# Strassen's scheme for the last product of a chain of attention and two MLPs

## The chip, the cores and the metric

One core of a Trainium2 chip runs the kernel. Time is the device time of one execution in microseconds (us); the median of the runs counts. TensorE multiplies, VectorE (DVE) and ScalarE (ACT) work on what comes out of it, GpSimd (POOL) helps early on, and SyncE (SP) issues the transfers.

## The reference, cut to what matters

```
x = attention(q, k, v, s)          # 2304 tokens, 512 wide
h = x @ moe_w_in                   # 2304 x 2048
x = (h * cos(h)) @ moe_w_out       # 2304 x 512
h = max(x @ w1, x @ w2, x @ w3)    # three products, 2304 x 768
out = h @ moe2_w_out               # 2304 x 512: the change is here
```

## The kernel before

A planner (class `Plan`) collects operations with an engine, a duration, a key, and the memory spans that they read and write; it plays them on a clock of its own and writes out each engine's instructions in the order of that play. On the chip each engine then works through its list in that order. POOL has nothing left to do in the stage of the change.

**The three products** `x @ w1`, `x @ w2`, `x @ w3` run as 27 groups, `GROUPS` = (fp, tp, m): fp is one of three pairs of d_ff chunks (128 wide), tp one of three pairs of token tiles (`TB` = 384 tokens), m the weight. I number them 0 to 26; fp is slowest, m fastest. Each is a 2 x 2 block product done by Strassen's scheme in 7 sub-products (`product`, L1341), each of 6 matmuls of 384 columns: two chunks of d_model times three terms, since every operand is kept as an f16 high half and an f16 low half (`halves`, L508: ACT writes the high one, DVE the low one). ACT copies three of the sub-products out of PSUM (`keep`), DVE forms the four quarters `q` of the result from banks and copies (`result`, L1375), and for m > 0 takes the maximum with what is there (L1379, L1370). The seventh sub-product of a group (`step_p4`) is placed after the second of the next group. A sub-product that opens no bank of its own adds to one whose earlier content was read first, so TensorE waits for that read.

**The last product** is before plain. When all three m of an (fp, tp) are done, `step_p4` splits the four quarters into halves: two ACT and two DVE instructions of 768 columns (L511 and L514). `final(i)` (L1297) makes 128 rows of the output from 18 matmuls of 512 columns, 6 chunks times 3 terms; there are 18 of them, the last cut in two column halves. A bank is copied out by ACT (`evac`, L904) with the output's scale, and SP stores it. The finals of the first two token pairs stand between the groups of fp = 2, the last eight behind the last group.

`w_operands` and `out_operands` make the weights' halves; `x_operands` the activations'. `combine` (L1120, its DVE instruction L1128) is one sum or difference of two f32 blocks.

Of the kernel before, what the change touches and what calls it, by code (L numbers as in the profile page):

```python
# [332 lines left out]
def attn_moe_kernel(ctx, tc, qT, kT, v, s, w_in, w_out, w1, w2, w3, wo2, out):  # L333
# [23 lines left out]
    def dspan(name, i=0):  # L357
        return (name, Plan.CELL * i, Plan.CELL * (i + 1))
# [750 lines left out]
    wo2_b = [w1_b.sub(2048 * f, 2048) for f in range(NC2)]  # L1109
    h2_b.update({(2, 0): w1_b.sub(2048 * NC2, HB), (2, 1): xo_b.sub(0, HB), (2, 2): xo_b.sub(HB, HB)})  # L1110
    assert 2048 * NC2 + HB <= WB and 2 * HB <= XB
    val2_b = Buf(nc, tail0, 2048 * NC2).ring(NC2)
    junk_b = Buf(nc, one_b.lo, 1024)
    ob_b = raw_all[0].ring(2)

    gate_scale()

# [82 lines left out]
    def out_values(key):  # L1200

        top, small = am_b[0], am_b[1]
        for f in range(NC2):
            rb = take("rw", raw_all)
            words = weight_load(wo2[f], 512, rb, key - LEAD)
            value, sp = value_of(words, 512, rb.span(), val2_b[f], key)
            vals.append((value, sp))
            col, unit = top.ap(F32, 8)[:, f:f + 1], mn_b[f // 2].ap(F32, 8)[:, 6:7]
            bound(value, sp, junk_b.ap(F16, 512), [junk_b.span()], col, top.span(), key)
            P.add("DVE", 0.07, key, lambda col=col, unit=unit: nc.vector.tensor_tensor(  # L1210
                out=col, in0=col, in1=unit, op=ALU.mult),
                reads=[top.span(), mn_b[f // 2].span()], writes=[top.span()])
        power(NC2, top, small, key, 7, margin=MARGIN)

    def out_operands(key):

        small = am_b[1]
        for f, (value, sp) in enumerate(vals):
            mb = mn_b[f // 2]
            by = mb.ap(F32, 8)[:, 5:6]  # L1220
            if f % 2 == 0:
                P.add("DVE", 0.07, key, lambda by=by, mb=mb: nc.vector.tensor_tensor(
                    out=by, in0=mb.ap(F32, 8)[:, 6:7], in1=small.ap(F32, 8)[:, 7:8], op=ALU.mult),
                    reads=[mb.span(), small.span()], writes=[mb.span()])
            d = wo2_b[f]
            halves(d.ap(F16, 512), d.ap(F16, 512, 1024), value, by, key, 512, [sp, mb.span(), dspan("w1")],
                   [d.span(0, 1024)], [d.span(1024, 1024)])
        for tp in range(3):
            a = sm_b[tp].ap(F32, 8)
            P.add("DVE", 0.07, key, lambda a=a: nc.vector.scalar_tensor_tensor(  # L1230
                out=a[:, 5:6], in0=small.ap(F32, 8)[:, 6:7], scalar=2.0 ** 20, in1=a[:, 6:7], op0=ALU.mult,
                op1=ALU.mult), reads=[sm_b[tp].span(), small.span()], writes=[sm_b[tp].span()])

    quarter = t_b[2].ap(F32, 8)[:, 2:3]
# [59 lines left out]

    pe3, fin_n = [3000], [0]

    def final(i, cuts=(0, 512)):  # L1297

        tp, tb, off = i // 6, i % 6 // 3, 128 * (i % 3)
        ob = take("ob", ob_b)  # L1300
        ot = ob.ap(F32, 512)
        for c0, c1 in zip(cuts, cuts[1:]):
            z = 6 + fin_n[0] % 2
            fin_n[0] += 1
            o = bank(z)[:, 0:c1 - c0]

            def last(c0=c0, c1=c1, o=o):
                for f in range(NC2):
                    wv = wo2_b[f].ap(F16, 1024).rearrange("p (a c) -> p a c", a=2)
                    hb = h2_b[f // 2, tp]  # L1310
                    at = (2 * (f % 2) + tb) * 2 * TB + 2 * off
                    hv = hb.ap(F16, 128, at), hb.ap(F16, 128, 8 * TB + at)
# [9 lines left out]
            sp = ob.span(4 * c0, 4 * (c1 - c0))
            evac(ot[:, c0:c1], o, 599, c1 - c0, [bspan(z), sm_b[tp].span()], [sp],
                 by=sm_b[tp].ap(F32, 8)[:, 5:6])
            r0 = 128 * i
            load(out[r0:r0 + 128, c0:c1], ot[:, c0:c1], 512 * (c1 - c0), 599, reads=[sp])
# [56 lines left out]
    def step_p4(st):  # L1383
        product(st, 3, st["b"], False)
        result(st, st["b"], 2, None)
        if st["m"] == 2:
            fp, tp, hf = st["fp"], st["tp"], st["hf"]
            hb = h2_b[fp, tp]
            for i in range(2):
                c = 2 * TB  # L1390
                halves(hb.ap(F16, c, 2 * c * i), hb.ap(F16, c, 8 * TB + 2 * c * i), hf.ap(F32, c, 4 * c * i),
                       2.0 ** -20, 590, c, [hf.span(4 * c * i, 4 * c)], [hb.span(2 * c * i, 2 * c)],
                       [hb.span(8 * TB + 2 * c * i, 2 * c)])

    old = None
    todo = []
    for g in range(len(GROUPS)):
        fp, tp, m = GROUPS[g]
        if tp == 0 and m == 0:
            if fp < 2:  # L1400
                todo = [(fp + 1, i, m_) for i in range(2) for m_ in range(3)]
        if todo and g % 9 >= 1:
            w_value(*todo.pop(0), 572 + 5 * fp)
            if not todo:
                w_operands(fp + 1, 573 + 5 * fp, 7)
        st = group_state(g)
        a, b, c, (e1, u2, e5) = st["a"], st["b"], st["c"], st["tmp"]
# [19 lines left out]
        if fp == 2 and tp >= 1 and m < 2:  # L1427
            for i in range(2):
                final(6 * (tp - 1) + 2 * m + i)
            if tp == 1 and m == 1:  # L1430
                final(4)
                final(5)
    step_p4(old)
    for i in range(10, 18):
        final(i, (0, 512) if i < 17 else (0, 256, 512))

    def busy(count, late):

# [140 lines left out]
```

## Time and profile before

| | |
|---|---|
| median of 3 runs | 824.15 us (823.35 to 827.08) |
| the profiled execution | 826.21 us |
| its span, first to last instruction | 824.6 us |
| mean granted TensorE clock | 0.998 |
| busy: TensorE, DVE, ACT, POOL | 800.1, 666.0, 563.6, 84.2 us |

The profile is of one execution. Its span leaves out what lies before the first and after the last instruction, so its own time is 1.6 us longer. Busy times are sums over the whole span; what bounds a stage is read from that stage.

### The profile page before, as it was taken

The page shows a single profiled execution, that of the slowest core. Times are in us where ns is not written, and L with a number is a line of the kernel's source. Part 1 is how long each engine was busy: PE and PEld are TensorE (multiplying, and loading weights), DVE is VectorE, ACT ScalarE, POOL GpSimd, SP SyncE. Part 2 cuts the span into 40 slices and gives each one's busy share as a digit, 9 for nine tenths or more (in the row PEclk, how much of TensorE's full clock was granted, in tenths as well). Part 3 has the DMA queues.
Part 4 walks back from the last instruction along what each step waited for, and adds up shares of the span by engine and source line. Part 5 has one row for each costly group of instructions (what it writes and reads, how often), then busy time and mean ns, then how long its engine had stood idle before and what let it go on. Part 6 is the DMA issues. An engine that isn't in the chain of part 4 may idle for free.

```text
span 824.6 us, 16555 instructions
## 1 busy us (share of the span) xinstructions
PE 800.1 (97%) x6058; PEld 511.8 (62%) x6058; DVE 666.0 (81%) x1613; ACT 563.6 (68%) x1242; POOL 84.2 (10%) x109
## 2 busy tenths in 40 slices
PE   8899989999999999999999979999999999999998
PEld 4567866788778777878544434444666666555554
DVE  6899999968996899678999999997999997513120
ACT  4788887988998878669998699964654544212221
POOL 4511122001101000000002620120000000000000
PEclk9999999999999999999999999999999999999999
DMA  8798999989999989956554134404004030010111
GB/s 223 164 227 188 207 266 206 227 193 222 248 199 195 233 198 227 269 182 197 155 151 133 34 89 130 126 6 149 1 27 128 5 98 1 1 52 27 39 49 66
DMA packets 154572, 114.16 MB, mean 138 GB/s; under 512 B 109662, under 2 KB 132446, under 8 KB 154492
## 3 DMA queue, kind: packets, MB, share of 16 engines
q1 hardware_dynamic: 154492, 113.11, 53.6%
q8 instruction: 47, 0.77, 0.4%
q14 instruction: 33, 0.27, 0.1%
HBM read 63.13 MB, written 23.74 MB: 105 GB/s over the span
## 4 chain that ended last, share of the span: by engine, by line
PE 44%; DVE 23%; ACT 3%; DMA 3%; issue 2%; SPq 0%; POOL 0%; DVEq 0%; POOLq 0%; ACTq 0%
PE banks L1350 21%; PE banks L933 9%; PE banks L1314 8%; DVE p L442 6%; DVE p L1260 3%; DVE p L1266 3%; DVE p L514 3%; PE banks L1277 2%; DVE p L731 2%; PE banks L784 1%; ACT p L412 1%; PE banks L718 1%; DVE p L1140 1%; DMA p<-in_moe_w_dram 1%; DVE p L462 1%
## 5 line engine op out<-in xcount | busy, mean ns | idle before, releaser
L933 PE MATMUL banks<-p,p 128*128 128x256 f16 (+1 forms) x1536 | 199.1, 286 | 1.4 <-ACT p L904 1.4
L1277 PE MATMUL banks<-p,p 128*128 128x512 f16 (+1 forms) x960 | 187.7, 358 | 4.2 <-DVE p L442 3.3
L1350 PE MATMUL banks<-p,p 128*128 128x384 f16 x1134 | 186.0, 326 | 1.0 <-DVE p L1375 0.7
L933 PEld LDWEIGHTS <-p 128*128 128x128 f16 x1536 | 145.8, 98 | 45.1 <-issue 7.0
L442 DVE SCALAR_TENSOR_TENSOR p<-p,p,p 128x512 f16<-128x512 f32 (+4 forms) x244 | 156.6, 667 | 11.7 <-ACT p L412 10.9
L412 ACT ACTIVATE p<-p,p 128x512 f16<-128x512 f32 (+4 forms) x242 | 142.5, 624 | 23.2 <-DVE p L745 5.9
L1350 PEld LDWEIGHTS <-p 128*128 128x128 f16 x1134 | 110.8, 98 | 75.2 <-issue 1.7
L1277 PEld LDWEIGHTS <-p 128*128 128x128 f16 x960 | 93.7, 98 | 97.2 <-issue 5.5
L904 ACT ACTIVATE p<-banks,p 128x256 f32<-128x256 f32 (+2 forms) x171 | 87.2, 523 | 91.4 <-PE banks L1314 61.6
L737 ACT ACTIVATE p<-p,p 128x128 f32<-128x128 f32 (+4 forms) x144 | 82.7, 576 | 5.7 <-DVE p L731 2.8
L1358 ACT ACTIVATE p<-banks 128x384 f32<-128x384 f32 x90 | 43.3, 486 | 50.7 <-PE banks L1350 50.6
L731 DVE CUSTOM_DVE_ANT_0 p<-banks,p 128x128 f32<-128x128 f32 (+4 forms) x144 | 71.7, 512 | 2.7 <-PE banks L722 1.3
L1375 DVE TENSOR_TENSOR p<-banks,p 128x384 f32<-128x384 f32 x81 | 44.4, 554 | 33.4 <-PE banks L1350 33.2
L1314 PE MATMUL banks<-p,p 128*128 128x512 f16 (+1 forms) x342 | 71.0, 368 | 0.0
L514 DVE SCALAR_TENSOR_TENSOR p<-p,p,p 128x512 f16<-128x512 f32 (+2 forms) x73 | 63.9, 901 | 4.9 <-ACT p L511 4.8
L511 ACT ACTIVATE p<-p,p 128x512 f16<-128x512 f32 (+2 forms) x73 | 54.8, 783 | 13.9 <-POOL p L1128 6.5
L1263 ACT ACTIVATE p<-p,p 128x512 f32<-128x512 f32 (+1 forms) x80 | 51.3, 670 | 12.3 <-DVE p L1260 12.3
L477 ACT ACTIVATE p<-p 128x512 f16<-128x512 f32 x61 | 38.1, 624 | 26.4 <-DVE p L465 22.7
L1314 PEld LDWEIGHTS <-p 128*128 128x128 f16 x342 | 33.5, 98 | 36.1
L1443 PE MATMUL banks<-p 128*128 128x384 bf16 (+1 forms) x321 | 49.6, 307 | 2.6 <-POOL p L576 1.1
L1266 DVE TENSOR_TENSOR p<-p,p 128x512 f32<-128x512 f32 (+1 forms) x80 | 50.6, 651 | 0.6 <-ACT p L1263 0.6
L718 PE MATMUL banks<-r,r 64*128 64x256 f32 (+3 forms) x360 | 47.7, 339 | 3.5 <-DVE p L731 2.5
(95 smaller groups left out, 821.7 us busy)
## 6 DMA issues: line engine op xcount, KB each, us to landing
p<-h_dram SPq DMA_DIRECT2D x64, 256.0 KB
p<-in_moe_w_out_dram SPq DMA_DIRECT2D x22, 512.0 KB
h_dram<-p SPq DMA_DIRECT2D x32, 320.0 KB
p<-in_moe_w_dram SPq DMA_DIRECT2D x18, 512.0 KB
p<-in_moe_w_in_dram SPq DMA_DIRECT2D x16, 512.0 KB
h_dram<-p SPq DMA_DIRECT2D x32, 256.0 KB
p<-in_k_dram SPq DMA_DIRECT2D x16, 288.0 KB
out_dram<-p SPq DMA_DIRECT2D x17, 256.0 KB
```

Source lines behind the costliest of these rows:

```text
L412: "ACT": (slow(cols, 0.19 if par else 0.09), lambda: nc.scalar.activation(out=out, in_=src, func=AF.Copy, scale=by)),
L442: n = P.add("DVEP", dve1(cols) + 0.06, key, lambda: nc.vector.scalar_tensor_tensor(out=lo, in0=src, scalar=by, in1=hi, op0=ALU.mult, op1=A ...
L514: P.add("DVEP", dve1(cols) + 0.06, key, lambda: nc.vector.scalar_tensor_tensor(out=lo, in0=src_, scalar=by, in1=hr, op0=ALU.mult, op1=ALU. ...
L718: nc.tensor.matmul(sp[:, o:o + kn], qq[rows_of[h], at:at + 128], kk[rows_of[h], k0:k0 + kn], start=(m == 0 and bool(opens)), stop=False)
L731: nc.vector.tensor_tensor_reduce(out=e, in0=sc, in1=km, op0=ALU.add, op1=ALU.min, scale=-0.125, scalar=3.0e38, accum_out=mn[:, j:j + 1]),
L737: "ACT", act(n, 0.28), tg, lambda j=j, e=e, mn=mn, sm=sm: nc.scalar.activation(out=e, in_=e, func=AF.Exp, scale=-1.0, bias=mn[:, j:j + 1], ...
L904: "ACT": (act(cols, 0.05 if by is None else 0.15), lambda: nc.scalar.activation(out=out, in_=src, func=AF.Copy, scale=1.0 if by is None el ...
L933: nc.tensor.matmul(hp, w[:, wp, ks], xx, start=(k == 0 and m == 0), stop=(k == KD - 1 and m == 2),)
L1266: P.add("DVEP", dve1(n), key, lambda ht=ht, lt=lt: nc.vector.tensor_tensor(out=lt, in0=lt, in1=ht, op=ALU.mult), reads=hs_ + ls_, writes=ls_)
L1277: nc.tensor.matmul(bank(base + d)[:, 0:n], w[:, wp, ds], xx, start=(c == 0 and z == 0), stop=(c == NC1 - 1 and z == 2))
L1314: nc.tensor.matmul(o, hv[hp], wv[:, wp, c0:c1], start=(f == 0 and m == 0), stop=(f == NC2 - 1 and m == 2))
L1350: nc.tensor.matmul(bank(z)[:, 0:TB], w_, x_, start=(opens and j == 0 and k == 0), stop=(j == 1 and k == 2), skip_group_check=True)
```

## The change

The last product is done by Strassen's scheme too: for each pair of token tiles and each 128 rows in it (`off`), 9 finals make 2 x 128 rows of output in 7 parts (`part`), of 9 matmuls with 256 columns each (3 pairs of d_ff chunks times 3 terms). The parts' results are joined by ACT (`times`, L1355, two per final) and DVE (`plus`, L1351, five per final).

The operands need sums: `h_operands` (L1311) makes for each (f, tp) four sums of 384 columns on DVE (L1136) and 7 half operands in place of 4 (ACT and DVE instructions of 768, 768 and 1152 columns). It stands only in the groups with fp = 2, where before two thirds of the splitting stood in those with fp < 2; the quarters of fp < 2 stay in f32 until then. The outputs for tp = 0 and tp = 2 share their memory. `out_operands` makes for each pair of chunks four sums of 256 columns and halves of 1024 and 768 columns in place of twice 512.

Finals 0 to 2 (tp = 0) go part by part between the sub-products of groups 24 to 26, in two banks; finals 3 to 8 stand behind the last group, in three banks each, taken in turn.

```diff
+    vals_b = Buf(nc, tail0, 2 * OB)
+    one_of = [vals_b, xo_b.part(0, 2 * OB), xo_b.part(2 * OB, 2 * OB)]
+    ho_b = {(f, tp): (one_of[f].part(0, OB), one_of[f].part(OB, OB)) for f in range(3) for tp in (0, 2)}
...
     def out_operands(key):
...
+            for o, x, y in ((t[0], v[1], v[0]), (t[1], v[3], t[0]), (t[2], v[2], t[1]), (v[1], v[3], v[1])):
+                combine(o, x, y, ALU.subtract, 256, key, False)
+            wb = w1_b.part(7168 * fp, 7168)
+            for i0, n, s_ in ((0, 4, v[0]), (4, 3, t[0])):
+                c = 256 * n
+                halves(wb.ap(F16, c, 512 * i0), wb.ap(F16, c, 3584 + 512 * i0), s_.ap(F32, c), by, key, c,
...
+    def h_operands(f, tp, key):
+
+        hf = hf_of[f, tp]
+        q, t = [hf.part(4 * TB * i, 4 * TB) for i in range(4)], sum_b
+        hi, lo = ho_b[f, tp]
+        for o, x, y, op in ((t[0], q[1], q[3], ALU.add), (q[1], q[0], q[1], ALU.subtract),
+                            (t[1], t[0], q[0], ALU.subtract), (t[2], q[2], t[1], ALU.subtract)):
+            combine(o, x, y, op, TB, key, False)
+        for i0, n, s_ in ((0, 2, q[0]), (2, 2, q[2]), (4, 3, t[0])):
+            c = n * TB
+            halves(hi.ap(F16, c, 2 * TB * i0), lo.ap(F16, c, 2 * TB * i0), s_.ap(F32, c), 2.0 ** -22, key, c,
...
+    def final(n, banks):
...
+        def part(i, o, os_, opens, closes):
+
+            def run():
+                for f in range(3):
+                    wb = w1_b.part(7168 * f, 7168)
+                    h = [z.ap(F16, 128, 2 * (TB * HOP[i] + 128 * off)) for z in ho_b[f, tp]]
+                    w = [wb.ap(F16, 256, 3584 * z + 512 * OOP[i]) for z in range(2)]
                     for m, (hp, wp) in enumerate(((0, 0), (0, 1), (1, 0))):
...
+                        nc.tensor.matmul(o, h[hp], w[wp], start=(opens and f == 0 and m == 0),
+                                         stop=(closes and f == 2 and m == 2), skip_group_check=True)
...
+        def first():
+            part(0, x, xs, True, False)
+            times(e1, e1s, x, xs)
+
+        def sixth():
+            part(5, y, ys, True, False)
+            plus(e2, e2s, y, ys, e1, e1s)
+
+        def second():
+            part(1, x, xs, False, True)
+            times(*row(0, 0), x, xs)
+
+        def fifth():
+            part(4, u, us, True, False)
+            plus(e5, e5s, u, us, e1, e1s)
+
+        def seventh():
+            part(6, y, ys, False, False)
...
+        def third():
+            part(2, u, us, False, True)
...
+        def fourth():
+            part(3, y, ys, False, True)
...
+        if banks[0] == banks[2]:
+            return [first, sixth, second, seventh, fifth, third, fourth]
+        return [first, sixth, fifth, second, seventh, third, fourth]
...
+        if beside:
+            beside.pop(0)()
...
-    for i in range(10, 18):
-        final(i, (0, 512) if i < 17 else (0, 256, 512))
+    last = None
+    for n in range(3, 9):
+        z = 3 * (n % 2)
+        for i, step in enumerate(final(n, (z, z + 1, z + 2))):
+            if i == 6 and n < 8:
+                last = step
+                continue
+            step()
+            if i == 0 and last:
+                last()
```

On TensorE the order up to group 24 stays, but for the place of three one-matmul steps; from group 24 on the matmuls of `product` (L1431, 384 columns) now alternate with those of `part` (L1343, 256 columns). On DVE, in the middle of group 24, before the change there are only the reads of group 23's and 24's own products, quarter by quarter (the names are buffers: p_6144 the quarters, p_1536 what stands for the maximum, p_4608 ACT's copies):

```order
L1375 TENSOR_TENSOR p_1536_7476<-banks,p_4608_7316 128x384
L1379 TENSOR_TENSOR p_6144_259<-p_1536_7476,p_6144_259 128x384
L514 SCALAR_TENSOR_TENSOR p_6144_281<-p_6144_259,p_6144_281 128x768
L1370 TENSOR_TENSOR p_6144_259<-banks,p_6144_259 128x384
L514 SCALAR_TENSOR_TENSOR p_6144_281<-p_6144_259,p_6144_281 128x768
L1375 TENSOR_TENSOR p_6144_257<-banks,p_4608_7313 128x384 x3
```

The same place after the change, from the fourth quarter of group 23 (L1453) on; L1351 are the joins of final 0 (the first is that behind its sixth part, the second that behind its fifth, which reads the bank that its third part adds to), L1458 the quarters of group 24, and L1136 with L514 are the operands h of (1, 1) and (2, 1):

```order
L1453 TENSOR_TENSOR p_6144_266<-banks,p_6144_266 128x384
L1351 SCALAR_TENSOR_TENSOR p_3072_267<-banks,p_32_101,p_3072_267 128x256
L1136 TENSOR_TENSOR p_4608_251<-p_6144_262 128x384
L514 SCALAR_TENSOR_TENSOR p_21504_255<-p_6144_262,p_21504_255 128x768
L1136 TENSOR_TENSOR p_6144_262<-p_6144_262 128x384
L1136 TENSOR_TENSOR p_4608_251<-p_4608_251,p_6144_262 128x384
L514 SCALAR_TENSOR_TENSOR p_21504_255<-p_6144_266,p_21504_255 128x768
L1458 TENSOR_TENSOR p_6144_264<-banks,p_4608_7304 128x384
L1136 TENSOR_TENSOR p_4608_251<-p_6144_262,p_4608_251 128x384
L1351 SCALAR_TENSOR_TENSOR p_3072_267<-banks,p_32_101,p_3072_267 128x256
L514 SCALAR_TENSOR_TENSOR p_21504_255<-p_6144_262,p_21504_255 128x768
```

What moved: between the quarters of one group and the next DVE now has the operands' sums and low halves, and joins on which TensorE waits stand behind them.

Also on DVE, behind the last group (the fourth quarter of group 26 is the L1453), the list begins with the low halves of h for (0, 2), (2, 2) and (1, 2), mixed with the joins of final 3:

```order
L1453 TENSOR_TENSOR p_6144_264<-banks,p_6144_264 128x384
L514 SCALAR_TENSOR_TENSOR p_10752_265<-p_6144_260,p_10752_265 128x768 x2
L1351 SCALAR_TENSOR_TENSOR p_2048_270<-banks,p_32_105,p_2048_270 128x256
L514 SCALAR_TENSOR_TENSOR p_21504_250<-p_6144_264,p_21504_250 128x768
L1351 SCALAR_TENSOR_TENSOR p_1024_271<-banks,p_32_105,p_2048_270 128x256
L514 SCALAR_TENSOR_TENSOR p_10752_265<-p_4608_251,p_10752_265 128x1152
L1351 SCALAR_TENSOR_TENSOR p_2048_273<-banks,p_32_105,p_1024_271 128x256
L1136 TENSOR_TENSOR p_4608_251<-p_6144_263 128x384
```

Before the change only two low halves of 768 columns stand there, and no join. p_10752_265 and p_21504_250 hold the operands of tp = 0 until final 2's fourth part has read them.

## Rows read from the trace of the kernel before

**Rows 1.** Windows: stretch, length, busy us (instructions) of each engine, clock, DMA share, GB/s.

```profile
675.00:700.00 25.00, 25.00 (x156) 15.09 (x155) 20.19 (x47) 12.96 (x26) 0.00 (x0) 1.00 0.05 20
716.00:744.00 28.00, 28.00 (x142) 13.74 (x141) 3.72 (x7) 5.40 (x9) 0.00 (x0) 1.00 0.10 38
771.00:791.00 20.00, 20.00 (x110) 10.62 (x109) 7.36 (x14) 4.33 (x8) 0.00 (x0) 1.00 0.07 27
```

**Rows 2.** The chain that ended last, 560 us to the end: start, us, what.

```profile
575.81 0.48 DVE p L1375
576.29 0.04 issue
576.33 1.14 PE banks L1350 x6
...
716.14 7.77 PE banks L1314 x36
723.91 6.83 PE banks L1350 x42
730.73 15.54 PE banks L1314 x72
...
759.92 7.77 PE banks L1314 x36
...
774.52 7.77 PE banks L1314 x36
...
789.11 3.88 PE banks L1314 x18
...
793.97 27.25 PE banks L1314 x144
821.23 0.02 issue
821.25 0.47 ACT p L904
```

**Rows 3.** Timeline of TensorE, 330 to 420 us: start, us, instructions of one line.

```profile
334.14 10.00 PE L933 MATMUL banks<-p,p 128*128 128x256 f16 x90
344.07 1.81 PE L784 MATMUL banks<-p,p 128*64 128x256 f16 x54
```

**Rows 4.** Groups by form from 566 us on: busy us, mean ns, idle before.

```profile
L1314 PEld LDWEIGHTS <-p 128*128 128x128 f16 x342 | 33.5, 98 | 36.1
L514 DVE SCALAR_TENSOR_TENSOR p<-p,p 128x768 f16<-128x768 f32 x18 | 17.2, 956 | 2.8 <-ACT p L511 2.8
L511 ACT ACTIVATE p<-p 128x768 f16<-128x768 f32 x18 | 15.1, 841 | 16.8 <-DVE p L1379 11.9 <-DVE p L1370 4.9
```

**Rows 5.** Timeline of DVE, four places: start, us, instruction.

```profile
583.85 0.61 DVE L514 SCALAR_TENSOR_TENSOR p<-p,p,p 128x384 f16<-128x384 f32 x1
584.38 0.55 DVE L1128 TENSOR_TENSOR p<-p 128x384 f32<-128x384 f32 x1
584.85 0.55 DVE L1375 TENSOR_TENSOR p<-banks,p 128x384 f32<-128x384 f32 x1
...
654.95 0.75 DVE L514 SCALAR_TENSOR_TENSOR p<-p,p,p 128x512 f16<-128x512 f32 x1
655.61 0.56 DVE L1375 TENSOR_TENSOR p<-banks,p 128x384 f32<-128x384 f32 x1
656.08 0.42 DVE L1128 TENSOR_TENSOR p<-p,p 128x256 f32<-128x256 f32 x1
656.41 0.42 DVE L1128 TENSOR_TENSOR p<-p 128x256 f32<-128x256 f32 x1
...
664.15 0.96 DVE L514 SCALAR_TENSOR_TENSOR p<-p,p 128x768 f16<-128x768 f32 x1
665.02 0.56 DVE L1370 TENSOR_TENSOR p<-banks,p 128x384 f32<-128x384 f32 x1
```

**Rows 6.** Timeline at the first final: the wait for the last product.

```profile
715.97 7.93 PE L1314 MATMUL banks<-p,p 128*128 128x512 f16 x36
716.17 0.56 DVE L1375 TENSOR_TENSOR p<-banks,p 128x384 f32<-128x384 f32 x1 [0.35 <-PE banks L1350]
```

More of the change, by code (lines that the diff above doesn't have):

```diff
@@ L1108, in attn_moe_kernel @@
     h2_b = {(i // 3, i % 3): Buf(nc, HB * i, HB) for i in range(6)}
[L1109 to L1112, printed above, removed]
+    OB = 7 * TB * 2
+    val2_b = [val_b[f // 2].part(2048 * (f % 2), 2048) for f in range(NC2)]
+    vals_b = Buf(nc, tail0, 2 * OB)
+    one_of = [vals_b, xo_b.part(0, 2 * OB), xo_b.part(2 * OB, 2 * OB)]
+    ho_b = {(f, tp): (one_of[f].part(0, OB), one_of[f].part(OB, OB)) for f in range(3) for tp in (0, 2)}
+    ho_b.update({(0, 1): (h2_b[0, 0], h2_b[1, 0]),
+                 **{(f, 1): (xo1_b.part(2 * OB * (f - 1), OB), xo1_b.part(2 * OB * (f - 1) + OB, OB))
+                    for f in (1, 2)}})
+    assert 4 * OB <= XB and 2 * OB <= 3 * 4096 and OB <= HB
+    keep_b = [Buf(nc, tail0 + 3 * 4096, 3072).parts(3), Buf(nc, wo_lo + 20 * 4 * TB, 2048).parts(2)
+              + [Buf(nc, tail0 + 3 * 4096 + 3072, 1024)]]
+    assert tail0 + 4 * 4096 <= tail1
     junk_b = Buf(nc, one_b.lo, 1024)
-    ob_b = raw_all[0].ring(2)
+    ob_b = raw_all[0].ring(2) + raw_all[1].ring(2)
     gate_scale()
@@ L1212, in out_values @@
                 reads=[top.span(), mn_b[f // 2].span()], writes=[top.span()])
-        power(NC2, top, small, key, 7, margin=MARGIN)
+        power(NC2, top, small, key, 7, 2.0 ** -12, MARGIN)
     def out_operands(key):
         small = am_b[1]
[L1218 to L1227, printed above, removed]
+        for fp in range(3):
+            mb = mn_b[fp]
+            by, bsp = mb.ap(F32, 8)[:, 5:6], [mb.span()]
+            P.add("DVE", 0.07, key, lambda by=by, mb=mb: nc.vector.tensor_tensor(
+                out=by, in0=mb.ap(F32, 8)[:, 6:7], in1=small.ap(F32, 8)[:, 7:8], op=ALU.mult),
+                reads=[mb.span(), small.span()], writes=[mb.span()])
+            v = [val_b[fp].part(1024 * i, 1024) for i in range(4)]
+            t = [ws4_b.part(1024 * i, 1024) for i in range(3)]
+            for o, x, y in ((t[0], v[1], v[0]), (t[1], v[3], t[0]), (t[2], v[2], t[1]), (v[1], v[3], v[1])):
[4 more added lines that the diff above has]
+                halves(wb.ap(F16, c, 512 * i0), wb.ap(F16, c, 3584 + 512 * i0), s_.ap(F32, c), by, key, c,
+                       [("sb", s_.lo, s_.lo + 4 * c)] + bsp, [wb.span(512 * i0, 2 * c)],
+                       [wb.span(3584 + 512 * i0, 2 * c)])
         for tp in range(3):
@@ L1230, in out_operands @@
             P.add("DVE", 0.07, key, lambda a=a: nc.vector.scalar_tensor_tensor(
-                out=a[:, 5:6], in0=small.ap(F32, 8)[:, 6:7], scalar=2.0 ** 20, in1=a[:, 6:7], op0=ALU.mult,
+                out=a[:, 5:6], in0=small.ap(F32, 8)[:, 6:7], scalar=2.0 ** 22, in1=a[:, 6:7], op0=ALU.mult,
                 op1=ALU.mult), reads=[sm_b[tp].span(), small.span()], writes=[sm_b[tp].span()])
@@ L1295, in attn_moe_kernel @@
     pe3, fin_n = [3000], [0]
[L1297 to L1312, printed above, removed]
+    def h_operands(f, tp, key):
[8 more added lines that the diff above has]
+            halves(hi.ap(F16, c, 2 * TB * i0), lo.ap(F16, c, 2 * TB * i0), s_.ap(F32, c), 2.0 ** -22, key, c,
+                   [("sb", s_.lo, s_.lo + 4 * c)], [hi.span(2 * TB * i0, 2 * c)], [lo.span(2 * TB * i0, 2 * c)])
@@ new lines, in final @@
+    def final(n, banks):
+        tp, off = n // 3, n % 3
+        x, y, u = (bank(z)[:, 0:256] for z in banks)
+        xs, ys, us = ([bspan(z)] for z in banks)
+        by, bsp = sm_b[tp].ap(F32, 8)[:, 5:6], [sm_b[tp].span()]
+        kb = keep_b[n % 2]
+        (e1, e2, e5), (e1s, e2s, e5s) = [k.ap(F32, 256) for k in kb], [[k.span()] for k in kb]
+        rows = [take("ob", ob_b) for _ in range(2)]
+        KEY = 560
+        def part(i, o, os_, opens, closes):
[4 more added lines that the diff above has]
+                    w = [wb.ap(F16, 256, 3584 * z + 512 * OOP[i]) for z in range(2)]
@@ L1322, in final, with plus @@
[L1322 to L1326, printed above, removed]
+            link("PE", 9 * mmh(256), pe3[0], run,
+                 reads=[z.span() for f in range(3) for z in ho_b[f, tp]] + [w1_b.span(0, 3 * 7168)], writes=os_)
+        def plus(to, ts, o, os_, e, es):
+            P.add("DVE", dve1(256), KEY, lambda: nc.vector.scalar_tensor_tensor(
+                out=to, in0=o, scalar=by, in1=e, op0=ALU.mult, op1=ALU.add), reads=os_ + es + bsp, writes=ts)
@@ new lines, in times, with row, store @@
+        def times(to, ts, o, os_):
+            P.add("ACT", slow(256), KEY, lambda: nc.scalar.activation(
+                out=to, in_=o, func=AF.Copy, scale=by), reads=os_ + bsp, writes=ts)
+        def row(tb, c):
+            return rows[tb].ap(F32, 256, 1024 * c), [rows[tb].span(1024 * c, 1024)]
+        def store(tb, c0, c1):
+            r0 = 128 * (6 * tp + 3 * tb + off)
+            load(out[r0:r0 + 128, c0:c1], rows[tb].ap(F32, c1 - c0, 4 * c0), 512 * (c1 - c0), 599,
+                 reads=[rows[tb].span(4 * c0, 4 * (c1 - c0))])
@@ new lines, in first @@
+        def first():
[12 more added lines that the diff above has]
+            part(6, y, ys, False, False)
+            if banks[0] != banks[2]:
+                plus(*row(1, 1), y, ys, e5, e5s)
@@ new lines, in third @@
+        def third():
+            part(2, u, us, False, True)
+            if banks[0] == banks[2]:
+                plus(*row(1, 1), y, ys, e5, e5s)
+            plus(*row(0, 1), u, us, e2, e2s)
+            if n < 8:
+                store(0, 0, 512)
+            else:
+                store(1, 256, 512)
+                store(0, 0, 512)
+        def fourth():
+            part(3, y, ys, False, True)
+            plus(*row(1, 0), y, ys, e1, e1s)
+            store(1, 0, 512 if n < 8 else 256)
@@ L1385, in step_p4 @@
         result(st, st["b"], 2, None)
[L1386 to L1393, printed above, removed]
+        if st["m"] == 2 and st["fp"] == 2:
+            if st["tp"] == 0:
+                h_operands(1, 0, 590)
+            if st["tp"] == 1:
+                h_operands(1, 1, 591)
+            h_operands(2, st["tp"], 592)
+    beside = []
     old = None
@@ L1406, in attn_moe_kernel @@
         st = group_state(g)
+        if g >= 24:
+            beside.extend(final(g - 24, (6, 7, 6)))
         a, b, c, (e1, u2, e5) = st["a"], st["b"], st["c"], st["tmp"]
@@ L1426, in attn_moe_kernel @@
         old = st
[L1427 to L1432, printed above, removed]
-    step_p4(old)
-    for i in range(10, 18):
-        final(i, (0, 512) if i < 17 else (0, 256, 512))
+        if fp == 2 and tp == 0 and m == 1:
+            h_operands(0, 0, 590)
+        if g == 22:
+            h_operands(0, 1, 591)
+        if g == 26:
+            h_operands(0, 2, 593)
+            h_operands(1, 2, 593)
+    step_p4(old)
+    last = None
[8 more added lines that the diff above has]
+                last()
     def busy(count, late):
```

12 lines of the change are left out of this document (4 added, 8 removed).

## The prediction

> **What bounds the kernel now.** I read the chain that ended last first [rows 2]. From 576.33 us to 821.23 us it is TensorE alone: DVE hands over once (575.81 to 576.29), then sub-products and finals follow each other to the end, and the last link is one ACT copy of 0.47 us. So in the stage of the change a microsecond of TensorE work is a microsecond of time, as long as nobody makes it wait. The windows say who could [rows 1]: from 675 to 700 us DVE is busy 20.19 of 25 us, from 716 to 744 us 3.72 of 28, from 771 to 791 us 7.36 of 20, ACT always less than 13 of 25. POOL does nothing. [...] So the change has to be costed twice: what TensorE saves, and whether DVE, which gets the new sums, still delivers in time.
>
> **TensorE.** The finals now are the six pieces on L1314: 7.77 + 15.54 + 7.77 + 7.77 + 3.88 + 27.25 = 69.98 us for 342 matmuls [rows 2]. Their pace at 512 columns is 15.54 / 72 = 0.2158 us; the last piece holds 108 of these and 36 of 256 columns, so the 36 took 27.25 - 108 x 0.2158 = 3.94, or 0.1095 us each. The stretch of 90 matmuls of 256 columns earlier in the kernel says (344.07 - 334.14) / 90 = 0.1103 [rows 3]. The new finals are 9 x 7 x 9 = 567 matmuls of 256 columns: at 0.1095, 62.1 us. That saves 7.9 us. Bounds: 62.5 by the longer pace, and 61.2 if a matmul of half the columns cost half of 0.2158: 7.5 to 8.8 us saved. The weight load of 98 ns [rows 4] fits under 109.5 ns, as it did in the stretch of 90. The 1134 matmuls of the products stay; their pace, 6.83 us for 42 [rows 2], is the clock for what follows.
>
> [...]
>
> **DVE: what is added.** Prices are distances from one start to the next in a full queue [rows 5]: a sum of 384 columns 584.85 - 584.38 = 0.47, of 256 columns 0.33 to 0.34; a low half of 768 columns 0.87; with a scale from memory 0.53 for 384 columns and 0.66 for 512, so 0.13 more for each 128. From that, estimates: 1152 columns 0.87 + 3 x 0.13 = 1.27; with a scale from memory 768 columns 0.92, 1024 columns 1.19, and the join of 256 columns 0.40. A join reads PSUM, which costs no more: the reads of banks in these rows take the same 0.55 as the sums in SBUF. The bounds of a join are 0.34, a sum of its size, and 0.53, the next longer row.
>
> One `h_operands` is 4 x 0.47 + 2 x 0.87 + 1.27 = 4.89 us, nine 44.0; `out_operands` 3 x (4 x 0.34 + 1.19 + 0.92) = 10.4; 45 joins 18.0; together 72.4 us. Gone are 18 low halves at 0.87 and 6 of 512 columns at 0.66, 19.7 us; 12 of the 18 stood in the first 18 groups. DVE gets 52.7 us more, and nearly all of it falls behind the start of group 18, 716.14 - 4 x 6.83 = 688.8 us. There it was idle most of the time, so the sum fits; what counts is the place. ACT gets 9 x 384 x 3 columns more and the 18 copies of finals become 18 shorter ones; at 0.84 us for 768 columns [rows 4] that is some 15 us in a stage where it is a third busy, and I cost it at nothing.
>
> **Where TensorE could wait.** Three places, each from the order and these prices.
>
> Groups 18 to 23 (688.8 to 729.8 us). A group's sum behind sub-product 7 must have read its bank before the next group's third sub-product adds to it, 2 x 0.976 = 1.95 us later. DVE starts 0.20 us after TensorE is through (715.97 to 716.17 [rows 6]) and holds 0.55; from its end to TensorE's start lie 0.04 (576.29 to 576.33 [rows 2]). So DVE may be 1.1 us behind. In these 41 us it has 34 sums and maxima (16.0), four `h_operands` (19.6) and the tail of the weights' (about 3.5): 39 us. Laid end to end in the printed order, never starting before the product that it reads, I find 0.4 to 1.1 us to spare at each, and 1.3 idle in group 21. It is 95% full, but it holds.
>
> Groups 24 to 26, where parts of 9 x 0.1095 = 0.985 alternate with sub-products of 0.976. Group 24 starts at 729.8, the third sub-product ends at 734.7, DVE's L1453 starts at 734.9. From there the second fence of the order: 0.47 + 0.40 + 0.47 + 0.87 + 0.94 + 0.87 = 4.0 to 738.9, just when the first quarter of group 24 is out (738.8); that and a sum that waits 0.12 for nothing but its predecessor's result end at 739.9. The join behind the fifth part could start at 739.8, so it is not late; it needs 0.48 + 0.04, and the third part, which adds to the same bank, comes at 740.6. That leaves 0.2 us. Finals 1 and 2 have the same gap, with DVE idle ahead of it.
>
> Behind the last group. `h_operands` (0, 2), (1, 2) and (2, 2) write where final 2 reads, so their low halves can't start before its fourth part ends, 729.8 + 21 x (0.976 + 0.985) = 771.0, plus 0.20 and an ACT half of 0.84: 772.0. DVE has then 9 low halves (9.0), 8 sums (3.8) and 11 joins (4.4), 17.2 us, done by 789.3 without waits, 790 with those on parts. Final 6 needs them at 772.0 + 21 x 0.985 = 792.7. So 2.7 us to spare, and still 1.3 with joins at their upper bound; finals 3 to 5 are the cover, and without it all 17.2 would show. The joins among them have a gap of two parts, 1.97 us, and 0.9 are enough, so they bear a low half of 0.87 ahead of them.
>
> So waits: between nothing and three times a low half ahead of the tight joins plus one missed sum, 3 x 0.87 + 0.9 = 3.5 us. I take 0.5, near the lower end, because each place has room by the same rows.
>
> **The first 18 groups** lose 12 x 0.87 = 10.4 us of DVE work. TensorE doesn't wait there now, so this gives nothing; weights of fp = 1 and 2 are ready sooner, which gives nothing either.
>
> **The end.** Before: an ACT copy of 256 columns, then the store of 128 KB, 824.6 - 821.72 = 2.9 us. After: a join of 256 columns, the same store. A store of 256 KB goes out about 1 us ahead of it now; if the last had to wait for all of it, 1.0 us. I take 0.1, bounds 0 and 1.0.
>
> **Sum.** 826.21 - 7.9 + 0.5 + 0.1 = 818.9 for an execution like the profiled one. That lies 2.06 above the median of its kernel, so for the median 824.15 - 7.3 = 816.85; I say 816.8. With the bounds: from -8.8 to -7.5 + 3.5 + 1.0 = -3.0, that is 815.4 to 821.2; the runs of before spread 0.8 below their median, so I let the range begin at 814.5.
>
> **The rivals.**
> - *DVE falls behind in groups 18 to 26.* For: it is 95% full there, and a queue in order lets one late instruction hold all behind it. Against: with 0.2 to 1.1 us to spare at each place, and 1.3 idle once. If its real pace is 6% slower than my prices, 55 us of work come 3.3 us late, TensorE stands as long, and with the tight joins some 4.5 us of the 7.9 are lost: 820.8. Within 0.5% (4.1 us) of before, which is about what a measurement of this kernel can tell from no change.
> - *The operands of the last three finals come late, and the kernel gets slower.* Place: the 17.2 us between the end of final 2 and final 6. The room is 2.7 us, then each microsecond counts; the gain is used up from 27.8 us of work on, 1.6 times my prices, and it is slower by 0.5% from 32. At twice the prices: 824.15 - 7.9 + 14.5 = 830.8. The rows would have to be far off for that.
> - *A matmul of 256 columns costs well over half of one of 512*, and the change is slower. Break-even is 69.98 / 567 = 0.1234 us; at a weight load and a half, 0.147, it ends at 837.5. Against: two places of this trace at 0.110. [...]
> - *Nothing comes of it*, since all is given back to waits: part of the first rival.
>
> **Chances.** The forecast 0.87 (faster by over 0.5%: below 820.0 us); DVE behind, or given back, within 0.5%, 0.08; slower by over 0.5% 0.05, of which 0.03 for the late operands and 0.02 for the small matmuls. The range is 814.5 to 821.0: it takes in the first rival's time and the bounds of the pace.
>
> **What would show it.** L1343 with 567 matmuls in about 62 us; the chain on TensorE from 576 us to about 813 us; group 24 starting at 730 and the finals behind the last group at 772; DVE over 90% busy from 690 to 744 and nearly idle in the last 20 us; idle time of TensorE on DVE under 1 us in total. Wrong would be: idle of TensorE before L1431 or L1343 released by L1351, L1458 or L514 of several us (first rival), a gap ahead of final 6 (second), or a pace of L1343 above 0.115 us.

## The result, and the profile after

The changed kernel takes 817.02 us (median of 6 runs, 815.77 to 818.47); the kernel before takes 824.91 us beside it (6 runs, 823.35 to 827.08). The ratio is 0.9904, 95% interval 0.9886 to 0.9922: faster by 7.9 us, where 7.35 were forecast. The profiled execution took 815.77 us.

The head of the page (busy us, share of the span, instructions) says what was paid for it:

```profile
span 814.0 us, 17135 instructions
PE 791.1 (97%) x6283; PEld 533.6 (66%) x6283; DVE 720.0 (88%) x1715; ACT 572.7 (70%) x1250; POOL 84.4 (10%) x109
```

DVE is busy 54 us longer than before, TensorE 9 us less. So the sums are not free; they have to be hidden. The chain that ended last (start, us, what) shows that they are:

```profile
573.37 0.48 DVE p L1458
573.85 0.04 issue
573.89 1.14 PE banks L1431 x6
...
675.67 52.65 PE banks L1431 x324
728.32 0.98 PE banks L1343 x9
729.31 0.97 PE banks L1431 x6
...
768.46 0.98 PE banks L1431 x6
769.43 41.28 PE banks L1343 x378
...
810.73 0.48 DVE p L1351
```

As before [rows 2], DVE hands over once and then TensorE works without a break: sub-products (L1431), 21 parts (L1343, 9 matmuls) alternating with sub-products, and the six finals behind the last group as one piece. The stage lasts 810.71 - 573.89 = 236.82 us; before it lasted 821.23 - 576.33 = 244.90. The difference is 8.08. The two spans differ by more, 10.6 us, because this execution came to the stage 2.44 us earlier. That part is chance: the instructions ahead of the stage are the same, the profiled execution is the fastest of the six, and in the seven experiments with a chain that reaches back there the stage starts between 574.89 and 576.98. So traces are compared below by the length of the stage, and kernels by their runs.

The windows of the stage (columns as in [rows 1]):

```profile
688.60:716.00 27.40, 27.40 (x171) 16.47 (x170) 25.61 (x45) 14.37 (x23) 0.00 (x0) 1.00 0.00 1
716.00:744.00 28.00, 28.00 (x198) 19.22 (x197) 26.90 (x47) 13.70 (x22) 0.00 (x0) 1.00 0.06 20
744.00:771.00 27.00, 27.00 (x211) 20.47 (x210) 17.44 (x33) 8.01 (x15) 0.00 (x0) 1.00 0.11 40
771.00:791.00 20.00, 20.00 (x186) 17.93 (x185) 17.54 (x30) 8.63 (x13) 0.00 (x0) 1.00 0.17 64
```

TensorE's busy time, right behind the length, fills each window, at a granted clock of 1.00. DVE's, the third of the busy times, is 25.61 of 27.4 and 26.90 of 28 us, 93 and 96%; in the second of these windows it was 3.72 before [rows 1]. Groups by form (busy us, mean ns of one, idle before) show how little idle time stands ahead of the new matmuls, 0.0 us, and how many there are:

```profile
L1343 PE MATMUL banks<-p,p 128*128 128x256 f16 x567 | 65.5, 273 | 0.0
L1351 DVE SCALAR_TENSOR_TENSOR p<-banks,p,p 128x256 f32<-128x256 f32 x45 | 21.5, 479 | 18.4 <-PE banks L1343 18.3
L514 DVE SCALAR_TENSOR_TENSOR p<-p,p 128x1152 f16<-128x1152 f32 x9 | 12.1, 1349 | 0.6 <-ACT p L511 0.6
```

The mean of 273 ns is how long one matmul lasts in this profile, and neighbours overlap; the pace is 41.28 / 378 = 0.1092 us. The joins wait 18.3 us for TensorE, TensorE none for them.

### The profile page after: what moved, and what is told of

Same layout as the page of the kernel before. It is cut to its first block, busy times and chain, and to the rows that moved or that the text cites. A ratio compares the mean times of both kernels' runs of the same rounds, so it can differ in the third digit from the quotient of the medians.

```text
span 814.0 us, 17135 instructions
## 1 busy us (share of the span) xinstructions
PE 791.1 (97%) x6283; PEld 533.6 (66%) x6283; DVE 720.0 (88%) x1715; ACT 572.7 (70%) x1250; POOL 84.4 (10%) x109
## 4 chain that ended last, share of the span: by engine, by line
PE 47%; DVE 36%; DMA 7%; ACT 5%; issue 4%; POOL 1%; SPq 0%; DVEq 0%; POOLq 0%; ACTq 0%
PE banks L1431 21%; PE banks L933 11%; DVE p L442 10%; PE banks L1343 8%; DVE p L1274 4%; DVE p L1280 4%; DVE p L514 3%; DVE p L731 3%; PE banks L718 3%; PE banks L784 2%; DMA p<-in_moe_w_dram 2%; ACT p L412 2%; DVE p L462 2%; DVE p L465 2%; DMA p<-in_q_dram 1%
## 5 line engine op out<-in xcount | busy, mean ns | idle before, releaser
L1291 PE MATMUL banks<-p,p 128*128 128x512 f16 (+1 forms) x960 | 187.7, 358 | 3.9 <-DVE p L442 3.1
L1431 PE MATMUL banks<-p,p 128*128 128x384 f16 x1134 | 188.6, 326 | 0.8 <-DVE p L1458 0.6
L933 PEld LDWEIGHTS <-p 128*128 128x128 f16 x1536 | 145.8, 98 | 45.1 <-issue 7.4
L1431 PEld LDWEIGHTS <-p 128*128 128x128 f16 x1134 | 110.8, 98 | 72.3 <-issue 1.5
L1291 PEld LDWEIGHTS <-p 128*128 128x128 f16 x960 | 93.8, 98 | 96.8 <-issue 5.0
L904 ACT ACTIVATE p<-banks,p 128x256 f32<-128x256 f32 (+2 forms) x152 | 74.5, 504 | 24.3 <-PE banks L933 22.1
L514 DVE SCALAR_TENSOR_TENSOR p<-p,p,p 128x512 f16<-128x512 f32 (+2 forms) x73 | 66.1, 929 | 6.0 <-ACT p L511 6.0
L511 ACT ACTIVATE p<-p,p 128x512 f16<-128x512 f32 (+2 forms) x73 | 56.9, 810 | 13.5 <-POOL p L1136 6.5
L1343 PE MATMUL banks<-p,p 128*128 128x256 f16 x567 | 65.5, 273 | 0.0
L1343 PEld LDWEIGHTS <-p 128*128 128x128 f16 x567 | 55.5, 98 | 8.8
L1458 DVE TENSOR_TENSOR p<-banks,p 128x384 f32<-128x384 f32 x81 | 43.9, 549 | 7.4 <-PE banks L1431 7.2
```

The lines of the kernel that those rows point to most:

```text
L904: "ACT": (act(cols, 0.05 if by is None else 0.15), lambda: nc.scalar.activation(out=out, in_=src, func=AF.Copy, scale=1.0 if by is None el ...
L933: nc.tensor.matmul(hp, w[:, wp, ks], xx, start=(k == 0 and m == 0), stop=(k == KD - 1 and m == 2),)
L1291: nc.tensor.matmul(bank(base + d)[:, 0:n], w[:, wp, ds], xx, start=(c == 0 and z == 0), stop=(c == NC1 - 1 and z == 2))
L1343: nc.tensor.matmul(o, h[hp], w[wp], start=(opens and f == 0 and m == 0), stop=(closes and f == 2 and m == 2), skip_group_check=True)
```

## The experiments

The theory: the whole gain is TensorE's, 567 matmuls at 0.1092 for 342 at the pace before; DVE's sums cost nothing as long as the low halves behind the last group are out 2.7 us ahead of final 6, and each microsecond past that costs one. The rivals: smaller matmuls have a price that something else pays back; the margin lies elsewhere than computed; the gain comes from how finals and sub-products are mixed. Durations of the stage are taken from the chain of each trace and set against 236.82 (after) or 244.90 (before).

**e1: only the smaller matmuls, in the kernel before.** All 18 finals are cut in two halves of 256 columns, 648 matmuls.

```diff
-    def final(i, cuts=(0, 512)):
+    def final(i, cuts=(0, 256, 512)):
...
-        final(i, (0, 512) if i < 17 else (0, 256, 512))
+        final(i)
```

> The kernel before with every plain final cut into two column halves, so 648 matmuls of 256 columns in place of 306 of 512 and 36 of 256: same number of columns, nothing else changed. Theory (a matmul of 256 columns costs 0.1093 us, TensorE alone sets this stage): the pieces on the finals' line sum to 648 x 0.1093 = 70.8 us against 69.98 before, and TensorE's chain gets 0.9 us longer. Rival (small matmuls cost well over half of large ones, by 0.1234 us or more each): 80 us or more, 10 us longer.

Measured: 826.23 us (one run; before 825.37, median of 13 runs on the same chip). Two of the six pieces on the finals' line in its chain:

```profile
729.99 15.72 PE banks L1314 x144
...
791.67 29.49 PE banks L1314 x270
```

All six sum to 70.76 us, 0.1092 each; the stage got 0.77 us longer, where the rival had 10 or more. A matmul of 256 columns takes 0.506 of one of 512 (0.1092 to 0.2158), so the rival is out.

**e2: each low half for the last three finals made twice.** This lays 6 x 0.87 + 3 x 1.27 = 9.0 us more on DVE where the margin should be 2.7.

```diff
+            if tp == 2:
+                a, b_, d = (z.ap(F16, c, 2 * TB * i0) for z in (hi, lo, hi))
+                P.add("DVEP", dve1(c) + 0.06, key, lambda a=a, b_=b_, s_=s_, c=c: nc.vector.scalar_tensor_tensor(
+                    out=b_, in0=s_.ap(F32, c), scalar=2.0 ** -22, in1=a, op0=ALU.mult, op1=ALU.subtract),
...
```

> The changed kernel with each DVE low half of h_operands for tp = 2 issued twice, 9.0 us more of DVE work behind the last group. Theory (DVE's list there is full from 769.9 to 787.2 us and final 6 comes at 789.9, so 2.7 us are to spare and then each microsecond counts): TensorE waits 6.3 us ahead of final 6 or spread over finals 3 to 6; time 817.0 + 6.3 = 823.3 us. Rival (DVE isn't near a limit, its work is hidden whatever it is): 817.0, no wait of TensorE.

Measured: 825.43 us (824.11 to 828.48, 10 runs), ratio to before 1.0004 (0.9986 to 1.0023): the gain is gone, and 2.1 us more than expected. TensorE's timeline behind the last group (start, us, instructions of one line, idle before and releaser; L1325 is the second low half, L1357 the joins):

```profile
770.56 19.81 PE L1349 MATMUL banks<-p,p 128*128 128x256 f16 x180
790.87 1.80 PE L1349 MATMUL banks<-p,p 128*128 128x256 f16 x15 [0.50 <-DVE p L1357]
794.86 0.39 PE L1349 MATMUL banks<-p,p 128*128 128x256 f16 x2 [2.19 <-ACT p L511]
796.90 2.10 PE L1349 MATMUL banks<-p,p 128*128 128x256 f16 x9 [1.65 <-DVE p L1325]
```

Then, from the chain of waits:

```profile
799.57 20.80 PE banks L1349 x172
```

In the chain the finals behind the last group start at 770.72 (the last sub-product at 769.75 and its 0.97). The 206 matmuls up to 799.57 would have taken 206 x 0.1092 = 22.5 us, so 6.35 us were lost up to there, to waits and to slow matmuls between them. What ends the last wait is the last low half on DVE:

```profile
798.15 1.36 DVE L1325 SCALAR_TENSOR_TENSOR p<-p,p 128x1152 f16<-128x1152 f32 x1
```

So operands do come late (the 2.19 us are for a high half that ACT could make only once DVE's sums were out), and 9.0 - 2.7 = 6.3 had been expected; that the two numbers agree is chance, as the account of the prediction below shows. The other 2.0 us come after the last wait: 172 matmuls in 20.80 us, 0.1209 each, where 18.8 is their time at 0.1092. The windows tell why (the clock is the number behind POOL):

```profile
792.00:796.00 4.00, 1.06 (x9) 0.47 (x6) 3.90 (x8) 1.82 (x2) 0.00 (x0) 1.00 0.35 131
796.00:799.50 3.50, 2.10 (x9) 1.16 (x9) 3.46 (x3) 0.66 (x2) 0.00 (x0) 0.58 0.00 0
799.50:802.00 2.50, 2.43 (x12) 1.75 (x13) 0.57 (x3) 0.00 (x0) 0.00 (x0) 0.50 0.00 0
802.00:804.00 2.00, 2.00 (x14) 1.51 (x13) 0.41 (x1) 0.26 (x1) 0.00 (x0) 0.66 0.00 0
804.00:806.00 2.00, 2.00 (x21) 1.78 (x20) 0.83 (x2) 0.21 (x1) 0.00 (x0) 1.00 0.00 0
```

TensorE was busy 1.06 of 4 us, then 2.10 of 3.5. The granted clock went from 1.00 to 0.50 and was back at 1.00 by 804 (0.58 and 0.66 are means over their stretches). The row of 2.5 us at 0.50 counts 12 matmuls, that of 2 us at 1.00 counts 21 (those across an edge of the window included). The clock had stood in no term of the prediction.

**e3: e2 with memory of its own.** On top of e2's edit, the operands (0, 2), which the list behind the last group begins with, no longer share memory with those of tp = 0.

```diff
+    ho_b[0, 2] = (h2_b[0, 1], h2_b[1, 1])
```

> The same doubled low halves, but the operands for (0, 2) get memory of their own (the quarters of (0, 1) and (1, 1), free by then), so that they can be made while DVE idles in groups 25 and 26. Theory (what counts is only the work that may not start before final 2 has read its operands): 6.0 us move ahead of the last group, 20.2 us stay in the 20.0 between, so TensorE waits 0 to 0.6 us; time 817.0 to 817.6. Rival (DVE's total decides): as with the memory shared, 823.

Measured: 817.03 us (815.34 to 819.57, 4 runs), ratio 0.9907 (0.9876 to 0.9939); the stage is 236.82 us, without a wait. One window, to be set beside that of after:

```profile
744.00:771.00 27.00, 27.00 (x209) 20.24 (x207) 24.37 (x44) 10.20 (x16) 0.00 (x0) 1.00 0.10 38
```

DVE does 24.37 us of work there in place of 17.44: a third of the operands moved ahead of final 2's end, into time in which DVE had been idle. So it is not the amount of work that cost 8.4 us in e2, but that it could not start while final 2 still read the memory.

**e8: e2 with TensorE kept busy.** e2's extra 2.0 us is blamed on the clock. If so, matmuls that serve nothing, put where TensorE would stand (57 of 256 columns into an unused bank, ahead of final 5's last part and of final 6), should give it back.

```diff
+        if n == 6:
+            def filler():
+                for _ in range(57):
+                    nc.tensor.matmul(bank(7)[:, 0:256], warm_b.ap(BF16, 128), w1_b.part(0, 7168).ap(BF16, 256),
+                                     start=True, stop=True)
+            pe3[0] += 1
+            link("PE", 57 * mmh(256), pe3[0], filler, reads=[warm_b.span(), w1_b.span(0, 512)], writes=[bspan(7)])
```

> The kernel with the doubled low halves in shared memory again, with 57 matmuls of 256 columns that serve nothing between finals 5 and 6, in a bank that nobody uses then, so that TensorE works (6.2 us) where it waited 6.3. Theory (of the 8.4 us that the doubled low halves cost, 6.3 are the wait and 2.0 the lower granted clock that follows it): TensorE's chain is 236.8 + 6.3 = 243.1 us, granted clock 1.00 to the end, time 823.3 us. Rival (the clock or the slow matmuls come from something else there, such as DVE and TensorE at one memory): 245.2 us as without the fillers, time 825.4.

Measured: 822.97 us (821.75 to 824.45, 10 runs; before 824.51, 13 runs), ratio 0.9983 (0.9970 to 0.9995). 823.3 had been expected. Stage 243.35 us, e2 had 245.19. Its windows, and the last piece of TensorE in its chain:

```profile
788.00:800.00 12.00, 12.00 (x113) 10.75 (x111) 11.86 (x16) 3.63 (x5) 0.00 (x0) 1.00 0.12 44
800.00:820.00 20.00, 19.32 (x176) 16.84 (x173) 7.70 (x16) 2.44 (x6) 0.00 (x0) 1.00 0.20 75
```

```profile
800.50 18.96 PE banks L1349 x172
```

The clock stays at 1.00, and the same 172 matmuls take 18.96 us for 20.80. That the price beyond the wait is the clock's is thereby shown in the traces. The times of e2 and e8 alone, on two chips, would hardly tell: their ratios differ by 0.0021, with intervals of 0.0012 to 0.0019 to either side. The mean granted clock of whole runs agrees: 0.992 to 0.996 in the ten of e2, 0.996 to 1.000 in the ten of e8.

**e5: the same margin from TensorE's side.** The last product's matmuls leave out the third pair of d_ff chunks (378 in place of 567), so final 6 comes 21 x 3 x 0.1092 = 6.9 us sooner after final 2, and DVE's work stays.

```diff
-                for f in range(3):
+                for f in range(2):
...
```

> The changed kernel with the third pair of d_ff chunks left out of the last product's matmuls: 378 in place of 567; all operands and joins are still made. Theory (TensorE is the bound until DVE's 17.2 us behind the last group no longer fit under finals 3 to 5): TensorE has 378 x 0.1093 = 41.3 us on the parts, 20.6 less; finals 3 to 5 take 13.8 us, the operands come 17.8 us after final 2, so TensorE waits about 4.0 us ahead of final 6; time 817.0 - 20.6 + 4.0 = 800.4 us. Rival (TensorE alone sets the time): 796.4, no wait.

Measured: 802.54 us (801.53 to 803.55, 4 runs), ratio 0.973 (0.9699 to 0.9760). TensorE's timeline behind the last group:

```profile
763.33 12.64 PE L1343 MATMUL banks<-p,p 128*128 128x256 f16 x114
776.37 0.81 PE L1343 MATMUL banks<-p,p 128*128 128x256 f16 x6 [0.41 <-DVE p L1351]
778.03 2.78 PE L1343 MATMUL banks<-p,p 128*128 128x256 f16 x24 [0.84 <-DVE p L1351]
782.49 0.82 PE L1343 MATMUL banks<-p,p 128*128 128x256 f16 x6 [1.68 <-ACT p L1355]
783.92 13.04 PE L1343 MATMUL banks<-p,p 128*128 128x256 f16 x102 [0.61 <-DVE p L1351]
```

A timeline's start lies 0.16 us ahead of the chain's (in e2 770.56 and 770.72). 763.33 + 0.16 + 150 x 0.1092 = 779.9, and the last piece starts at 783.92: 4.0 us lost, the number expected, but not in the way expected. Final 6 reads here the operands (0, 2) and (1, 2), and none of the waits is for one of these; (2, 2) is read by no matmul of this kernel. TensorE waits for banks: three times for a join, and 1.68 us for an ACT copy that stood behind ACT's last high half, which had waited for DVE's sums:

```profile
780.91 1.16 ACT L511 ACTIVATE p<-p 128x1152 f16<-128x1152 f32 x1 [0.61 <-DVE p L1136]
781.99 0.46 ACT L1355 ACTIVATE p<-banks,p 128x256 f32<-128x256 f32 x1
```

So it is DVE's long list here too, but through the reads of banks that stand in the queues behind the operands' work. The expectation had both sides too early: the last wait ends 783.92 - 763.49 = 20.4 us behind the start of final 3, where 17.8 were taken, and the 150 matmuls ahead of it are 16.4 us, where 13.8 were. The rest is again the clock:

```profile
783.90:786.00 2.10, 2.08 (x13) 1.57 (x13) 0.84 (x2) 0.00 (x0) 0.00 (x0) 0.63 0.00 0
786.00:788.00 2.00, 2.00 (x12) 1.44 (x11) 0.48 (x1) 0.45 (x1) 0.00 (x0) 0.54 0.20 77
788.00:790.00 2.00, 2.00 (x21) 1.80 (x19) 1.25 (x3) 0.02 (x1) 0.00 (x0) 1.00 0.27 100
```

The last piece in the chain takes 13.06 us for 102 matmuls, 1.9 more than at 0.1092. Together 5.9 us, so the time is 2.1 above the 800.4 expected.

**e6: nothing interleaved.** All nine finals stand behind the last group, in three banks each; the operands for tp = 2 are made after final 2.

```diff
...
-        if g >= 24:
-            beside.extend(final(g - 24, (6, 7, 6)))
...
-    for n in range(3, 9):
+    for n in range(9):
         z = 3 * (n % 2)
+        if n == 4:
+            for f in range(3):
+                h_operands(f, 2, 593)
```

> The changed kernel with finals 0 to 2 behind the last group like the others, in three banks each, and nothing between the sub-products of groups 24 to 26; the operands for tp = 2 are made once final 2 has read those for tp = 0. Theory (TensorE has the same matmuls, DVE's work still fits under them): TensorE's chain from its start near 574 us to its end is as long as in the changed kernel, 236.8 us, within 0.5. Rival (the alternation of parts and sub-products is what pays, or what keeps DVE in time): some microseconds longer, with waits ahead of the first finals.

Measured: 818.03 us (one run; before 824.13), with the stage at 812.89 - 576.07 = 236.82 us again:

```profile
677.85 72.15 PE banks L1431 x444
...
752.94 59.95 PE banks L1343 x549
```

The mixing of finals and sub-products brings nothing by itself, and the tight places that it made cost nothing either.

**e4 and e7: a late join in finals 0 to 2.** The join behind the fifth part, which has some 0.2 us to spare, is done three times. In e4 as three operations of the planner:

```diff
             part(4, u, us, True, False)
-            plus(e5, e5s, u, us, e1, e1s)
+            for _ in range(3 if banks[0] == banks[2] else 1):
+                plus(e5, e5s, u, us, e1, e1s)
```

> The changed kernel with the join behind the fifth part issued three times in finals 0 to 2, where the third part adds to the same bank after one sub-product of 0.98 us. Theory (the join starts 0.20 us after the part, TensorE goes on 0.04 us after its end, so one join of 0.48 us leaves 0.25 us): three joins end 0.20 + 0.39 + 0.39 + 0.48 + 0.04 = 1.50 us after the part and TensorE waits 0.52 us ahead of each of the three third parts, 1.6 us in all. Rival (the read isn't what the third part waits for, or there is more room): no wait.

Measured: 817.94 us (one run; before 824.13), stage 236.82 us, no wait. Its chain shows that the edit did not reach the place it was meant for:

```profile
739.38 4.87 PE banks L1432 x30
...
747.19 3.93 PE banks L1343 x36
```

Where after has one sub-product and one part in turn, here five sub-products stand in a row, and later four parts: the planner reckoned with the longer join and put the third part elsewhere. This run says nothing of what a late join costs. In e7 the three are one operation to the planner, at the duration of one, so the order stays:

```diff
...
-            plus(e5, e5s, u, us, e1, e1s)
+            plus(e5, e5s, u, us, e1, e1s, 3 if banks[0] == banks[2] else 1)
```

> As in the run before with the join issued three times, but with the planner told of one, so that the order of TensorE's list stays that of the changed kernel and the third part stands one sub-product behind the fifth. Theory: three joins end 0.20 + 0.39 + 0.39 + 0.48 + 0.04 = 1.50 us after the fifth part, TensorE comes after 0.98, so it waits 0.52 us in each of finals 0 to 2: chain 236.8 + 1.6 = 238.4 us. Rival (that read isn't what the third part waits for): 236.8, no wait.

Measured: 821.36 us (one run; before 824.51), stage 816.39 - 576.98 = 239.41, 2.6 more than after. Timeline of both engines at final 0:

```profile
740.30 1.52 DVE L1351 SCALAR_TENSOR_TENSOR p<-banks,p,p 128x256 f32<-128x256 f32 x3
...
741.87 1.14 PE L1343 MATMUL banks<-p,p 128*128 128x256 f16 x9 [0.68 <-DVE p L1351]
```

```profile
744.00:774.00 30.00, 28.56 (x220) 21.28 (x219) 21.05 (x39) 8.32 (x15) 0.00 (x0) 1.00 0.10 38
```

The waits of the third parts are 0.68, 0.72 and 0.72 us, 2.1 in the waits' view; by TensorE's timeline these parts start 0.84, 0.88 and 0.89 us late, 2.6 together, so a stop costs some 0.17 beyond the wait that is listed. Expected were 1.6, 0.52 at each place: 0.26 of what is more at each is that three joins in one place take 1.52 us and not 1.26. So the tight place is where the prediction put it. The window holds two of these stops, with work between them, and the clock is 1.00 in it; from 738 to 744 us, around the first, it is 1.00 too.

## Why the prediction was right

- **TensorE, 62.1 us for the finals.** 567 x 0.1092 = 61.9, against 69.98 [rows 2]: 8.06 of the 8.08 us by which the stage is shorter. The 0.1095, got from 36 matmuls as a remainder, was 0.0003 high; e1 measured the same pace without the rest of the change.
- **DVE, 52.7 us more, hidden.** 720.0 - 666.0 = 54.0 busy. The prices that were estimated hold; only ACT got less than the 15 us that were costed at nothing, 572.7 - 563.6 = 9.1. In the timeline of after, a join stands 0.39 us ahead of the next (estimated 0.40) and a low half of 1152 columns 1.27 (estimated 1.27):

```profile
737.22 0.47 DVE L1351 SCALAR_TENSOR_TENSOR p<-banks,p,p 128x256 f32<-128x256 f32 x1
737.61 0.95 DVE L514 SCALAR_TENSOR_TENSOR p<-p,p 128x768 f16<-128x768 f32 x1
...
785.87 1.35 DVE L514 SCALAR_TENSOR_TENSOR p<-p,p 128x1152 f16<-128x1152 f32 x1
787.14 0.47 DVE L1351 SCALAR_TENSOR_TENSOR p<-banks,p,p 128x256 f32<-128x256 f32 x1
```

- **The first two places.** Groups 18 to 26: no wait. Group 24 starts one sub-product ahead of the first part, 728.32 - 0.98 = 727.34, or 729.8 with the 2.44 us by which the stage began sooner; forecast was 729.8. The join behind final 0's fifth part ends at 737.69 and the third part starts at 737.95, which with 0.04 of hand-over leaves 0.2 us, as forecast; e7 shows that the third part waits for that join.

```profile
737.95 1.15 PE L1343 MATMUL banks<-p,p 128*128 128x256 f16 x9
```

- **Behind the last group: the times right, the room wrong.** The finals there start at 769.43, 771.9 on before's clock (forecast 772), and the last low half ends at 787.2, 17.8 us later (forecast 18.0). The prediction set this against final 6's first matmul, 21 parts in. In the kernel's list final 6 begins after 20 parts, and the last low half, of 1152 columns for (2, 2), is read first by the 207th matmul: the 180, final 6's first part, final 5's last, and 8 of final 6's sixth part stand ahead. That is where e2's last wait stands (180 + 15 + 2 + 9 = 206). In after it starts at 769.43 - 0.16 + 206 x 0.1092 = 791.8, so the last low half had 4.5 us to spare, not 2.7. A join had less: the one at 787.14, right behind the last low half, reads the bank of final 5's fifth part, and the third part, which adds to that bank, starts behind 171 matmuls, at 787.9. The join ends at 787.6, so 0.3 us were left, the tightest there; the prediction had these joins with a low half of 0.87 us ahead of them, not one of 1.27. No run tries that place by itself.
- **Why e2 and e5 still gave the expected waits.** That is luck. In e2 the last wait ends 28.85 us behind the start of final 3, where 18.0 + 9.0 = 27.0 were reckoned, mostly since 15 joins stand ahead of the last low half and not 11 as in after; and the 206 matmuls ahead of its reader are 22.5 us, where 189 of them, 20.7, were reckoned. Both sides are 1.8 us too early, and their difference comes out. In e5 they are 2.6 too early, and what TensorE waits for is another thing.
- **Waits, 0.5.** This was the mis-sized term: in the stage there were none. The tail, 0.1, was not there either (3.4 us from TensorE's end to that of the span before, 3.3 after). Without both terms the forecast would have been 7.9 us faster, which is what the runs measured.
- **DVE behind.** It did not come to it: DVE was 93 to 96% full, as forecast, and TensorE never waited for it, so the room was enough.
- **Operands late.** The mechanism is real, as e2 shows; its room of 2.7 us is not what the runs show. Its price was too low: "then each microsecond counts" left out that the pause also took the granted clock down, to 0.50 in e2 and to a mean of 0.54 over 2 us in e5, worth 2.0 us in e2 and 1.9 in e5. So the gain was used up sooner than at the 27.8 us of work that the forecast said: e2, with 17.2 + 9.0 = 26.2, already ends level with before.
- **Small matmuls.** Refuted by e1: 0.1092 against a break-even of 0.1234.

That the stage is shorter by TensorE's own work alone is shown by its chain, by e1 and by e6. Not tried was how full DVE can get in groups 18 to 23 before TensorE waits there.

## What to carry to other kernels

Where one engine's work fills the stage end to end, cost a change as two sums: what that engine saves, and for each thing it will read, when the engine that makes it is done; the second sum needs distances between starts in a full queue, not durations (a join of 0.47 us stands 0.39 ahead of the next instruction in after). Set each end against the first instruction that reads it, and look at what stands behind the new work in the same queue: here a join had 0.3 us left where the operands had 4.5. An experiment that gives the expected number can do so in another way (e5), so read what ended each wait. A limit that comes from shared memory goes away with a buffer (e3), and a planner can go round an experiment (e4), so read the order before believing that an edit did nothing. If TensorE will stand for some microseconds, count time at a lower granted clock afterwards as well: here 2.0 us behind 6.35 lost (e2) and 1.9 behind 4.0 (e5).

## What the runs showed of the hardware that was not expected

- After waits of 0.50, 2.19, 1.65 and 0.57 us within 9 us, with little work between them, the granted clock was 0.50 from 799.5 to 802 us and 1.00 again from 804 on; this cost 2.0 us (e2), in e5, at 0.63 and 0.54 from 783.9 to 788 us, 1.9 us. Three stops of 0.84 to 0.89 us, 14.6 us apart, left it at 1.00 (e7), and with the wait filled it stayed there (e8).
- Three joins of 256 columns that write the same place take 1.52 us, 0.52 from start to start; in after a join of that size stands 0.39 us ahead of the next instruction.
